# The order table of a one-core attention and MLP kernel, with its first three fifths ordered anew

## The chip, the core and the metric

The kernel runs on one core of one Trainium2 chip. The metric is the device time of one execution in microseconds (us). Five engines work side by side, each taking its own instructions strictly in the program's order: PE (TensorE, matmuls), ACT (ScalarE), DVE (VectorE), POOL (GpSimd, which here also issues one queue of transfers) and SP (SyncE, which issues the other transfers). They wait for each other by semaphores. The granted clock of PE is 1.00 in the profiled execution.

## The reference

q, k and v have shape (8, 8, 576, 64): 8 batches, 8 heads, 576 positions, 64 features. The attention is linear, and its output is the input x of a two-layer MLP with 4608 tokens, 512 inputs and 2048 hidden units.

```
q_s = softmax of q over its features
k_s = softmax of k over the positions
kv  = einsum('bhsd,bhse->bhde', k_s, v)
x   = einsum('bhsd,bhde->bhse', q_s, kv), reshaped to (4608, 512)
h   = x @ w_in
g   = h * tanh(softplus(h))
out = g @ w_out
```

## The kernel before

**What it computes, in which parts.** Item i (0 to 31) is a pair of heads of one batch; items 4b to 4b+3 make the 512 inputs of batch b. The first 512 positions of a batch are one column block of x, and the 64 left over from each of the 8 batches make a ninth. Every matmul of the MLP is done as three with operands split in a high and a low part (high by high, high by low, low by high), so each operand is first cast (high part) and then subtracted (low part).

Column blocks 0 to 2 go through the plain MLP. n = 0 to 47 is 16 hidden blocks for each of the three: `H` (four parts, or `HM`, all four) makes the first layer in bank ph, `Y` the activation, `G` or `GA` the high part gh (on DVE or on ACT), `GL` the low part gl (on DVE), `O` or `OP` the second layer in the banks po. Column blocks 3 to 8 go through it two at a time, in three passes k = 0, 1, 2, with seven products for eight: `A k.n.p` is product p (1 to 7) of hidden block n of the first layer (banks px, py, pz), `BB k.f.p` the same of the second layer (banks qx, qy, qz), six matmuls per step for `A` and six for `BB`. `C` copies a bank out on ACT (L860), `J` adds a bank to such a copy on DVE (L864), `N` is the activation. A bank is free for the next product when its `C`, `J` or `N` is done.

**Weights.** `R j` loads a weight tile; `RA`, `RM` or `RL` or `RS`, `RB`, `RC`, `RH` and `RO` or `RD` turn it into its high and low part on ACT, POOL and DVE. For the passes with seven products, weights are mixed (`WW`, `WM`), split (`WH`, `WL`) and put into the DRAM tensor ws by transfers on SP (`WP`, `WK`). `F e` fetches two of them back with one transfer of 512 KB on the POOL queue (L815) into one of six ring slots.

**Attention.** `LK`, `LQ` and `V` load k, q and v on SP. `MK` and `KA` take the maximum of k (DVE) and subtract it (ACT), `KT` transposes k on PE, `EK` is its exponential (ACT). `MQ`, `SQ`, `EQ`, `Q`, `QZ` and `QM` make the softmax of q on DVE, POOL, ACT, DVE, DVE and POOL; `T` transposes it and `TC` copies it out. `KP` multiplies k by v (`PK` later, together with the tails), `S` scales the product into kvt, `XP` or `PX` multiplies q by kvt. `ZT` copies the tail of an item out on ACT, `ST` stores it. `FI n` puts n fill matmuls on PE, whose results nobody reads; they stand at the start alone.

**What sets the order.** There is no scheduler. The string ORDER (L23 to L154) lists 2551 tokens, such as `KT1he` or `A0.2.7`: a step, its numbers, and letters that name its banks. The loop at L970 issues the steps one after the other, and what each issues stands on its engines' queues in that order. So a token's place decides what it stands behind on each of its engines, and its letters decide which bank it waits for.

```
for token in ORDER.split():
    name, numbers, letters = re.fullmatch("([A-Z]+)([0-9.]*)([a-z]*)", token).groups()
    stages[name](*(int(x) for x in numbers.split(".") if x), *([letters] if letters else []))
```

Of the kernel before, what the change touches and what calls it, by code (L numbers as in the profile page):

```python
# [24 lines left out]
V3 MQ2 FI1g FI9a EK1 R2 QZ0 SQ2 MK2 EQ1 V2 Q1 KA2 QM0 EQ2 KT2hd R3 QZ1 RA0b MQ3 QM1 R7 T0ge EK2 Q2 FI4a RM0 R10 SQ3
TC0 T1fc RB0 R4 KP0a QZ2 TC1 RC0 EQ3 QM2 R5 RA1d S0 RM1 LK4 MK3 XT0bc RH0 XP0ha Q3 KA3 R6 RL2 RD0 ZT1 KT3ef Z0 QZ3 R8
T2gc EK3 RB1 QM3 TC2 ZL0 KP2f LQ4 ZT0 RC1 Z1 RL3 ZL1 RH1 T3he PP RA2g S2 H0c TC3 ST1 RB2 RO1 H1 RA3d XP2ha RC2 R9 RB3
RH2 XT2eg H4b RC3 RO2 Z2 R11 Z3 H5 ZL2 RH3 RL7 ZL3 H6 RA7f L4 RM4 H8a MK4 ZT3 ZT2 RA4d RL5 H2 RD3 LK6 RA5g H3 LK5 RB4
RA6h H7 RL6 RC4 H9 R13 RB5 H12e Y0 R14 RC5 RL8 Y1 V4 H10 RB6 RA8d H13 RB7 RH5 R12 H11 RC6 GA0 RO5 H14 GL0 Y2 LQ5 RB8
H15 RH4 RL10 GA1 MQ4 H16h R17 Y3 RC8 H17 GA2 RO4 R16 GL1 RH6 H18 GL2 RA9g H19 RO6 RM9 RC7 O0 GA3 MK5 R19 Y4 RL13 R15  # L30
RB9 RA10f GL3 RM11 RH7 RC9 RA11e O1 RB10 RO7 RH9 RB11 RM14 RC10 RO9 GA4 RC11 RH8 R21 RH10 LK7 GL4 RO8 H20g R20 RH11
MQ5 RA13h B4e H21 KS4 RO10 RM12 H22 RA12f H23 SQ5 RB13 H24e RB12 SQ4 H25 RC12 EK4 H26 RC13 R23 RL16 EQ4 R22 H27 ST2
RH13 Q4 KP4fh EQ5 R24 RS17 R18 R30 O2 RO13 S4 ST0 Y5 R31 MK6 RO11 RA17f V6 RM15 G5 RH12 RB17 RL19 O3 Y6 RC17 RA14h GL5
# [1002 lines left out]
```

## Time and profile before

| what | before |
|---|---|
| median of 3 runs | 793.56 us (793.13 to 794.63) |
| the profiled execution | 795.84 us |
| its span, first to last instruction | 794.1 us |
| instructions in the span | 12637 |
| DMA | 178.85 MB, mean 225 GB/s |
| granted clock of PE | 1.00 in every stretch of 20 us but the last, partly empty one (0.94) |

The span leaves out what lies before the first and after the last instruction; 1.8 us of the profiled execution lie outside it. Times below are counted from the span's start. In rows of the timeline, the first number is the start in us, the second the length, then engine, line, operation, what is written and read, the shape, the count, and in brackets the idle time of the engine just before it and what ended it. A row of the waits has the waiting engine and line, what it waited for, the time in total, how often, and the longest.

### The profile page before, as it was taken

Reading aid. Unit: us, or ns where it says so; the run is one execution under the profiler, and the core shown is the slowest. Engines: PE = TensorE matmul, PEld = TensorE weight load, DVE = VectorE, ACT = ScalarE, POOL = GpSimd, SP = SyncE. Lnnn points to the kernel's source line nnn. Section 1 sums busy time; section 2 is a strip of 40 time slices with the busy share of each in tenths; the row PEclk is TensorE's granted clock in tenths of the full one; section 3 lists DMA queues with packets and bytes.
Section 4 is the critical chain, followed back from the end, with each engine's and each line's share of the span. In section 5 each row is a group of like instructions: output and inputs, shape, how many; then the busy total and the mean of one; then the engine's idle time right before and its main releaser. Section 6 shows DMA issues by size and latency. Waiting matters only on the chain.

```text
span 794.1 us, 12637 instructions
## 1 busy us (share of the span) xinstructions
PE 781.2 (98%) x4640; PEld 632.7 (80%) x4640; DVE 539.0 (68%) x877; ACT 498.4 (63%) x946; POOL 277.1 (35%) x350
## 2 busy tenths in 40 slices
PE   8999999999999999989999999999999999999997
PEld 7788868788878778867778788778878888888886
DVE  6997976777676778654789885335897822257854
ACT  6998857667685767379885653769654513446351
POOL 6998621432424444345232113412211212112111
PEclk9999999999999999999999999999999999999999
DMA  9994556847493556789766657785857776657576
GB/s 338 405 355 162 200 170 208 295 139 228 159 308 128 188 184 208 256 279 281 253 199 231 218 188 236 224 273 158 274 181 229 228 222 212 206 165 236 163 236 185
DMA packets 76684, 178.85 MB, mean 225 GB/s; under 512 B 15568, under 2 KB 28112, under 8 KB 76624
## 3 DMA queue, kind: packets, MB, share of 16 engines
q0 software_dynamic: 24768, 90.19, 35.7%
q1 hardware_dynamic: 51712, 87.74, 32.6%
q8 instruction: 36, 0.59, 0.3%
q14 instruction: 24, 0.20, 0.1%
q10 hardware_dynamic: 144, 0.13, 0.0%
HBM read 138.19 MB, written 39.85 MB: 224 GB/s over the span
## 4 chain that ended last, share of the span: by engine, by line
PE 86%; ACT 5%; DVE 3%; DMA 3%; issue 2%; POOL 0%; SPq 0%; DVEq 0%; ACTq 0%; POOLq 0%
PE ph L645 15%; PE po L683 14%; PE px L832 13%; PE qx L849 12%; PE qz L849 8%; PE qy L849 8%; PE py L832 7%; PE pz L832 3%; DMA ws<-m_out 2%; PE pt L567 1%; PE px L532 1%; DMA q<-in_q_dram 1%; ACT g L868 0%; DVE g L864 0%; ACT q L464 0%
## 5 line engine op out<-in xcount | busy, mean ns | idle before, releaser
L815 POOL DMA_DIRECT2D ws<-ws x172 | 92.8, 542 | 330.3 <-PE px L832 65.7
L882 ACT CAST gs<-g 128x1024 fp32r<-128x1024 f32 x84 | 86.9, 1050 | 70.4 <-PE qx L849 35.2
L832 PE MATMUL px<-xh,ws 128*128 128x512 f32 x384 | 129.7, 391 | 0.7 <-ACT g L860 0.6
L218 DVE TENSOR_TENSOR gs<-g,gs 128x1024 fp32r<-128x1024 f32 x84 | 102.1, 1232 | 34.1 <-ACT gs L882 34.1
L683 PE MATMUL po<-wo,gh 128*128 128x512 f32 x384 | 119.8, 393 | 0.0
L849 PE MATMUL qx<-gs,ws 128*128 128x512 f32 x432 | 101.8, 390 | 0.0
L849 PEld LDWEIGHTS qx<-gs,ws 128*128 128x128 f32 x432 | 80.8, 188 | 18.4 <-issue 1.6
L645 PE MATMUL ph<-xs,wi 128*128 128x512 f32 x384 | 92.5, 391 | 0.0
L860 ACT COPY g<-px 128x512 f32<-128x512 f32 x72 | 41.5, 586 | 75.7 <-PE px L832 75.6
L832 PEld LDWEIGHTS px<-xh,ws 128*128 128x128 f32 x384 | 72.1, 188 | 17.9 <-ACT g L860 1.8
L683 PEld LDWEIGHTS po<-wo,gh 128*128 128x128 f32 x384 | 71.1, 188 | 17.3 <-issue 1.6
L645 PEld LDWEIGHTS ph<-xs,wi 128*128 128x128 f32 x384 | 71.6, 188 | 16.0 <-ACT xt_first L617 0.8
L683 PE MATMUL po<-wo,gl 128*128 128x512 f32 x192 | 75.0, 391 | 0.0
L832 PE MATMUL px<-xl,ws 128*128 128x512 f32 x192 | 74.7, 389 | 0.0
L864 DVE TENSOR_TENSOR g<-py,g 128x512 f32<-128x512 f32 x48 | 32.7, 686 | 55.3 <-PE py L832 37.4
L832 PE MATMUL py<-xh,ws 128*128 128x512 f32 x192 | 66.8, 390 | 2.1 <-DVE g L864 2.1
L849 PE MATMUL qz<-gs,ws 128*128 128x512 f32 x288 | 67.5, 389 | 0.0
L849 PE MATMUL qy<-gs,ws 128*128 128x512 f32 x288 | 67.4, 389 | 0.0
L849 PEld LDWEIGHTS qy<-gs,ws 128*128 128x128 f32 x288 | 54.1, 188 | 11.2
L849 PEld LDWEIGHTS qz<-gs,ws 128*128 128x128 f32 x288 | 54.0, 188 | 11.2
L218 POOL TENSOR_TENSOR q<-q,qm 128x576 f32<-128x576 f32 (+1 forms) x32 | 39.2, 1227 | 54.3 <-DVE qm L377 32.9
L218 DVE TENSOR_TENSOR g<-g,g 128x1024 f32<-128x1024 f32 x48 | 57.3, 1214 | 0.2
(166 smaller groups left out, 1380.2 us busy)
## 6 DMA issues: line engine op xcount, KB each, us to landing
ws<-ws POOLq DMA_DIRECT2D x172, 512.0 KB, 4.6
v<-in_v_dram SPq DMA_DIRECT2D x14, 594.0 KB, 6.1
ws<-m_in SPq DMA_DIRECT2D x32, 256.0 KB, 3.0
ws<-m_out SPq DMA_DIRECT2D x32, 256.0 KB, 3.7
...
```

Source lines behind the costliest of these rows:

```text
L218: eng.tensor_tensor(out, a, b, ALU.subtract)
L532: nc.tensor.matmul((px, pt)[x][h][o], kvt[a, j], at[e + j]["qT"][x][a], start=True, stop=True)
L567: nc.tensor.matmul(pkv[i][j * D:(j + 1) * D], k, v_two[a, j, c], start=c == 0, stop=c == NR - 1)
L645: nc.tensor.matmul(gs[n], wi[f][:, a, t], x[:, z], start=t == 0 and i == 0, stop=t == HP - 1 and i == 2)
L683: nc.tensor.matmul(po[t], g[a][:, t * P:(t + 1) * P], wo[f][:, z], start=f == 0 and i == 0, stop=f == NF - 1 and i == 2)
L815: nc.gpsimd.dma_start(t.rearrange("p s z j c -> p s (z j c)"), ws[e % (NW // 2)].bitcast(F32R))
L832: nc.tensor.matmul(dst, w[:, a, j], xc[k, p][z][:, j].rearrange("p b s -> p (b s)"), start=p in (1, 2, 7) and j == 0 and i == 0, stop=j == ...
L849: nc.tensor.matmul(psb[key, k][m], w[:, a, m], g[:, z, f % 2], start=first and i == 0, stop=f == NH - 1 and i == 2, skip_group_check=p in ...
L860: nc.scalar.copy(g_quad(k, n)[q], psb[1, k, n])
L864: nc.vector.tensor_tensor(g, psb[2 if q == 0 else 7, k, n], g, ALU.add)
L882: nc.scalar.copy(t[:, 0], gq[k, h][G_PART[p]])
```

## The change

The string ORDER is replaced; nothing else is. Both strings have 2551 tokens. They hold the same steps with the same numbers, but for 69 tokens. Most of these have other bank letters. Twelve move the high part of a hidden block between engines (eight from DVE to ACT, four from ACT to DVE), and twelve move a step of the weights' conversion to another engine (`RL`, `RM`, `RS` for each other, `RO` and `RD` for each other). The last 446 tokens stand as before, and of the tokens before them nearly all stand elsewhere. The first lines of the string and of its common part show the kind of the difference:

```diff
-FI1h FI12a LK0 LQ0 LK1 LQ1 EX LQ2 LK2 LQ3 R0 LK3 MQ0 V0 V1 MK0 SQ0 MK1 R1 KA0 MQ1 KT0db EQ0 FI3a KA1 SQ1 Q0 EK0 KT1he
...
+FI1g FI1e FI9g LK0 LQ0 LK1 LQ1 EX LQ2 LK2 LQ3 MK0 V0 R0 KA0 KT0ba V1 MQ0 FI3c FI12f R1 MK1 SQ0 KA1 R2 MQ1 EQ0 KT1hg V2
...
```

The new string has one line more, so a line of the kernel's code is L(n+1) where it was L(n).

**PE at the start.** Its first rows before: fills (idle), then the transposes of k of items 0, 1 and 2 (pk, pkt), with fills in between.

```order
L407 MATMUL idle_127<-ident 128x128 x12
L435 MATMUL pk_171<-ident,kt_140 128x128 x4
L436 MATMUL pkt_172<-ident,kt_140 64x128
L407 MATMUL idle_179<-ident 128x128 x3
L435 MATMUL pk_189<-ident,kt_144 128x128 x4
L436 MATMUL pkt_190<-ident,kt_144 64x128
L407 MATMUL idle_199<-ident 128x128
L407 MATMUL idle_201<-ident 128x128 x9
```

The same rows of the change:

```order
L408 MATMUL idle_127<-ident 128x128
L408 MATMUL idle_129<-ident 128x128 x9
L436 MATMUL pk_159<-ident,kt_139 128x128 x4
L437 MATMUL pkt_160<-ident,kt_139 64x128
L408 MATMUL idle_169<-ident 128x128 x3
L408 MATMUL idle_173<-ident 128x128 x12
L436 MATMUL pk_196<-ident,kt_143 128x128 x4
L437 MATMUL pkt_197<-ident,kt_143 64x128
L408 MATMUL idle_206<-ident 128x128 x4
```

The twelve fills stand behind the first transposes now, and the group of one and nine that stood behind the second transposes stands ahead of the first.

**DVE between its work for ph12 and ph14**, ahead of KP6 on PE, which takes the bank of ph14. Before, from the low part of hidden block 12 to that of 14:

```order
L218 TENSOR_TENSOR gl12_1290<-ph12_1193,gh12_1279 128x512
L485 TENSOR_SCALAR qs6_1272,total6_1297<-qs6_1272 128x10
L486 RECIPROCAL qs6_1272<-qs6_1272 128x10
L377 TENSOR_TENSOR km8_1186<-km8_1186,kw8_1253 128x4
L485 TENSOR_SCALAR qs7_1260,total7_1306<-qs7_1260 128x10
L486 RECIPROCAL qs7_1260<-qs7_1260 128x10
L218 TENSOR_TENSOR gl13_1309<-ph13_1197,gh13_1300 128x512
L490 TENSOR_TENSOR q6_1058<-q6_1058,qs6_1272 128x640
L663 CAST gh14_1325<-ph14_1222 128x512
L263 SCALAR_TENSOR_TENSOR wc_out14_1295<-wc_out14_1295,raw_x_105 128x512
L218 TENSOR_TENSOR gl14_1332<-ph14_1222,gh14_1325 128x512
```

The same stretch of the change, with the five rows ahead of it:

```order
L742 TENSOR_TENSOR w_in1_1272<-wi1_90 128x512
L742 TENSOR_TENSOR w_in1_1272<-wi9_98 128x512
L264 SCALAR_TENSOR_TENSOR wc_out14_1259<-wc_out14_1259,raw_x_105 128x512
L271 SCALAR_TENSOR_TENSOR wc_out14_1259<-raw_x_105,wc_out14_1259 128x512
L219 TENSOR_TENSOR gl12_1298<-ph12_1206,gh12_1291 128x512
L491 TENSOR_TENSOR q6_1021<-q6_1021,qs6_1237 128x640
L476 TENSOR_REDUCE qs7_1318<-q7_1087 128x10
L486 TENSOR_SCALAR qs7_1318,total7_1327<-qs7_1318 128x10
L487 RECIPROCAL qs7_1318<-qs7_1318 128x10
L219 TENSOR_TENSOR gl13_1332<-ph13_1195,gh13_1323 128x512
L219 TENSOR_TENSOR gl14_1335<-ph14_1227,gh14_1325 128x512
```

The cast gh14, the join of km8, the reciprocal of q6 and a weight step no longer stand between gl12 and gl14; two weight steps and w_in1 stand ahead of gl12.

**DVE ahead of the product py of hidden block 4 in pass 0** (A0.4.7), whose bank is that of block 2 and is free when both additions from py0_2 are done (J). qm24 is the maximum of item 24, whose load is LQ24. Before:

```order
L377 TENSOR_TENSOR qs23_4073<-qs23_4073,sz23_4091 128x18
L485 TENSOR_SCALAR qs23_4073,total23_4106<-qs23_4073 128x18
L486 RECIPROCAL qs23_4073<-qs23_4073 128x18
L386 TENSOR_REDUCE qm24_4122<-q24_4075 128x18
L864 TENSOR_TENSOR g0_1_0_3921<-pz0_3_4018,g0_1_0_3921 128x512
L864 TENSOR_TENSOR g0_1_2_3923<-py0_2_3892,g0_1_2_3923 128x512
```

The change:

```order
L865 TENSOR_TENSOR g0_1_3_3921<-py0_2_3906,g0_1_3_3921 128x512
L458 STREAM_TRANSPOSE k24_4111<-kt_two_114 128x576
L865 TENSOR_TENSOR g0_2_0_4079<-pz0_4_4113,g0_2_0_4079 128x512
L865 TENSOR_TENSOR g0_1_2_3920<-py0_2_3906,g0_1_2_3920 128x512
L387 TENSOR_REDUCE qm24_4151<-q24_4075 128x18
```

The addition from py0_2 stands ahead of the maximum of item 24 now, where it stood two rows behind it.

**Fetches.** Two places of the string, from a fetch to the step that first reads it. Before, with BB0.3.1 the first that reads F30 and BB0.5.2 the first that reads F36:

```
F30 GK0.1.0 N0.1.3 A0.6.3 C0.7.2 T25 MS26 GX0.0.0v A0.7.5 N0.6.1 J0.7.0 A0.6.4 GX0.0.1v N0.7.0 N0.1.2 C0.7.3 MT26 BB0.0.1 SQ26
F32 BB0.1.1 GX0.1.0v F33 GK0.1.2 EQ26 BB0.2.1 F34 LQ27 J0.7.3 ST22 BB0.3.1
F36 J0.7.2 N0.7.3 F35 GX0.3.0v QW26 F37 PK24df GK0.2.1 N0.5.2 KB28 PX24cb J0.6.2 GH0.2.2 BB0.6.1 QV26 N0.6.3 MQ27 N0.4.3
GK0.2.2 BB0.0.2 N0.6.2 XR25 GX0.2.0v N0.7.2 BB0.1.2 MS27 MT27 BB0.7.1 SQ27 GH0.7.0 XR24 GK0.7.0 BB0.2.2
...
```

The change:

```
F33 T25 F30 S24 F31 BB0.0.1 F32 J0.6.2 EQ26 GK0.1.3 BB0.1.1 C0.7.3 LQ27 GK0.1.2 BB0.2.1 Q26 BB0.3.1
F39 XR25 GK0.2.2 MS27 F36 BB0.2.2 XR24 T26 KB28 GK0.2.3 BB0.3.2 XH1.1 F40 GX0.1.1v GH0.7.0 BB0.4.2 KM28 GH0.7.1 GK0.7.0 BB0.5.2
```

More of the change, by code (lines that the diff above doesn't have):

```diff
@@ L23 @@
 ORDER = """
-FI1h FI12a LK0 LQ0 LK1 LQ1 EX LQ2 LK2 LQ3 R0 LK3 MQ0 V0 V1 MK0 SQ0 MK1 R1 KA0 MQ1 KT0db EQ0 FI3a KA1 SQ1 Q0 EK0 KT1he
[L25 to L33, printed above, removed]
@@ L89 @@
-EQ25 A0.6.6 F26 LQ26 Q25 WP15.0 PS GH0.1.1 J0.4.2 A0.5.4 U26.0 N0.4.1 A0.5.3 J0.5.2 C0.6.2 GK0.1.1 QW25 A0.6.5 F29
-N0.4.2 J0.6.0 N0.5.0 QV25 A0.6.7 GH0.1.2 U26.1 N0.1.0 MQ26 LK28 A0.7.1 N0.0.0 F28 V26 A0.7.2 C0.7.0 GH0.1.0 A0.7.7 F31
-C0.6.3 QM25 N0.2.3 J0.6.3 N0.0.3 A0.7.6 N0.6.0 F30 GK0.1.0 N0.1.3 A0.6.3 C0.7.2 T25 MS26 GX0.0.0v A0.7.5 N0.6.1 J0.7.0
-A0.6.4 GX0.0.1v N0.7.0 N0.1.2 C0.7.3 MT26 BB0.0.1 SQ26 F32 BB0.1.1 GX0.1.0v F33 GK0.1.2 EQ26 BB0.2.1 F34 LQ27 J0.7.3
-ST22 BB0.3.1 Q26 N0.5.3 MK28 GH0.1.3 BB0.4.1 N0.5.1 GX0.1.1v GH0.2.0 A0.7.4 GH0.2.1 GK0.2.0 A0.7.3 GK0.1.3 BB0.5.1
@@ L94 @@
-N0.7.1 F36 J0.7.2 N0.7.3 F35 GX0.3.0v QW26 F37 PK24df GK0.2.1 N0.5.2 KB28 PX24cb J0.6.2 GH0.2.2 BB0.6.1 QV26 N0.6.3
-MQ27 N0.4.3 GK0.2.2 BB0.0.2 N0.6.2 XR25 GX0.2.0v N0.7.2 BB0.1.2 MS27 MT27 BB0.7.1 SQ27 GH0.7.0 XR24 GK0.7.0 BB0.2.2
-F39 DP0.0.0 F38 DP0.0.1 KM28 GH0.2.3 QM26 BB0.3.2 F40 GX0.2.1v BB0.4.2 GH0.7.1 GK0.2.3 BB0.5.2 F41 GX0.3.1v BB0.6.2
-T26 GK0.7.1 BB0.7.2 EQ27 BB0.0.7 GH0.7.2 Q27 LQ28 GX0.0.2v BB0.1.7 GH0.7.3 F43 F42 GX0.1.2v BB0.2.7 GH0.6.0 GK0.7.2
-QW27 BB0.3.7 GK0.7.3 XH1.1 BB0.4.7 GH0.6.1 GX0.2.2v BB0.5.7 GX0.3.2v F45 F44 GK0.6.0 BB0.6.7 GH0.6.2 GX0.0.3v BB0.7.7
@@ L99 @@
-F46 DJ0.0.0 BB0.0.6 GK0.6.1 QV27 BB0.1.6 GK0.6.2 BB0.2.6 GH0.3.0 DJ0.0.1 QM27 DS0.0.1 GH0.6.3 BB0.3.6 ST23 F47 F48 V28
-GK0.6.3 DS0.0.0 BB0.4.6 GH0.5.0 GK0.3.0 BB0.5.6 F49 GX0.2.3v BB0.6.6 GH0.5.1 S26 T27 ZT24 UE28.1 BB0.7.6 F50 GX0.1.3v
-BB0.0.3 DP0.2.0 MQ28 ZT25 DP0.2.1 GK0.5.0 UE28.0 BB0.1.3 GH0.5.2 XL1.1 PX26df GH0.5.3 GK0.5.1 BB0.0.5 XR26 U28.0 XR27
-XA1.0v XH1.3 BB0.1.5 F52 GK0.5.2 BB0.2.5 GH0.3.1 XA1.1v BB0.3.5 F53 GK0.5.3 F51 BB0.4.5 GH0.3.2 U28.1 GX0.3.3v XH1.5
-BB0.5.5 GK0.3.1 BB0.6.5 XL1.5 BB0.7.5 GK0.3.2 BB0.2.3 DP0.1.0 GH0.3.3 BB0.3.3 F56 XH1.2 GK0.3.3 F54 DP0.1.1 F55
@@ L104 @@
-BB0.4.3 XL1.3 GH0.4.0 XH1.7 DJ0.3.1 BB0.5.3 F57 XL1.2 BB0.6.3 GH0.4.2 XL1.7 GH0.4.1 BB0.7.3 GK0.4.2 F58 DJ0.3.0 A1.0.2
-GH0.4.3 DJ0.1.0 DS0.3.0 ST24 MS28 GK0.4.0 PK26df GK0.4.1 A1.0.1 XA1.2v BB0.0.4 GK0.4.3 XH1.6 BB0.1.4 C1.0.0 XL1.6 F59
-BB0.2.4 DJ0.1.1 J1.0.0 MT28 BB0.3.4 F60 SQ28 A1.0.7 F62 EQ28 Q28 LQ29 BB0.4.4 LK30 XA1.3v DS0.3.1 BB0.5.4 F61 A1.0.6
-A1.1.1 C1.0.2 XH1.4 A1.0.5 XL1.4 BB0.6.4 C1.0.3 S28 MQ29 BB0.7.4 F64 J1.0.3 MS29 F63 MK30 A1.0.3 QW28 F65 C1.1.0
-DJ0.2.0 A1.0.4 QV28 A1.1.6 J1.0.2 A1.1.2 C1.1.2 KB30 A1.1.5 J1.1.0 F66 DJ0.2.1 A1.2.7 MT29 C1.1.3 QM28 F68 A1.2.1 KM30
@@ new lines @@
+EK0 FI4e MQ2 SQ1 LK3 EK1 Q0 SQ2 V3 EQ1 MK2 R3 QZ0 KA2 Q1 QM0 EQ2 KT2de R4 RM0 QZ1 R5 MQ3 RA0h QM1 T0fb EK2 RB0 LK4
+RA1d Q2 SQ3 T1ag RM1 RC0 KP0e TC1 QZ2 TC0 RB1 R8 EQ3 RL2 S0 RH0 MK3 R6 XT0cb XP0ha R7 Q3 KA3 QM2 ZT1 ZT0 KT3fg QZ3 R10
+Z0 RD0 T2bc EK3 RC1 QM3 Z1 KP2f ZL0 TC2 ZL1 RA2g R9 RL3 T3hd PP RH1 S2 H0c TC3 RB2 R11 H1 RA3a RO1 RC2 RM4 XP2he RB3
+ST1 RH2 RC3 RO2 R13 XT2df H4b Z2 ZT3 H5 Z3 ZL2 RL5 LQ4 ZT2 RA4g ZL3 H2 RH3 RB4 H3 RA5f L4 MK4 RL8 H8e RC4 H6 LQ5 RD3
+RL6 H7 Y0 RB5 RA6h H9 LK6 RC5 RA7a H10 RL7 LK5 RB6 GA0 H12f RH5 GL0 RA8d H11 R15 RC6 RO5 RH4 R12 H13 RB8 Y1 H14 R30
@@ new lines @@
+A0.7.2 WP15.0 PS GH0.1.0 ZT23 N0.3.0 LK28 N0.6.0 A0.5.4 ST23 GH0.1.1 F28 ST22 MQ26 A0.7.1 C0.6.3 V26 J0.5.2 N0.4.3
+J0.6.3 MS26 A0.6.3 GK0.1.1 C0.7.0 N0.5.0 A0.6.4 GK0.1.0 N0.4.2 GH0.1.2 J0.7.0 A0.7.6 N0.5.1 MT26 SQ26 N0.6.1 N0.7.0
+A0.7.7 C0.7.2 QM25 GH0.1.3 A0.7.5 F33 T25 F30 S24 F31 BB0.0.1 F32 J0.6.2 EQ26 GK0.1.3 BB0.1.1 C0.7.3 LQ27 GK0.1.2
+BB0.2.1 Q26 BB0.3.1 J0.7.3 QW26 QV26 A0.7.3 GX0.1.0v N0.6.2 A0.7.4 N0.6.3 MK28 QM26 N0.1.3 N0.5.2 F34 BB0.4.1 GX0.0.0v
+N0.5.3 F35 N0.0.3 N0.7.3 BB0.5.1 GX0.0.1v F37 N0.2.2 N0.7.1 MQ27 BB0.6.1 N0.2.3 J0.7.2 GH0.2.0 GX0.3.0v BB0.7.1 N0.7.2
@@ new lines @@
+F38 N0.3.2 GK0.2.0 PK24df GH0.2.3 GX0.3.1v DP0.0.0 PX24cb DP0.0.1 GX0.2.0v GH0.2.1 BB0.0.2 GH0.2.2 GK0.2.1 BB0.1.2 F39
+XR25 GK0.2.2 MS27 F36 BB0.2.2 XR24 T26 KB28 GK0.2.3 BB0.3.2 XH1.1 F40 GX0.1.1v GH0.7.0 BB0.4.2 KM28 GH0.7.1 GK0.7.0
+BB0.5.2 F41 ZT24 MT27 GX0.2.1v BB0.6.2 GK0.7.1 GH0.7.2 BB0.0.7 SQ27 BB0.1.7 F42 GX0.1.2v GX0.0.2v BB0.2.7 EQ27 UE28.0
+LQ28 GK0.7.2 BB0.3.7 GH0.6.0 GX0.2.2v BB0.4.7 GH0.6.1 GK0.6.1 BB0.7.2 F45 F44 GK0.6.0 BB0.5.7 GH0.7.3 F43 GK0.7.3
+BB0.0.6 GH0.6.2 ZT25 GX0.3.2v BB0.6.7 Q27 BB0.1.6 U28.0 F46 QW27 XL1.1 BB0.7.7 QV27 GK0.6.2 BB0.2.6 GH0.6.3 GH0.3.0
@@ new lines @@
+GK0.6.3 BB0.3.6 MQ28 QM27 BB0.4.6 S26 F47 DJ0.0.1 BB0.5.6 F48 T27 DJ0.0.0 BB0.6.6 GH0.5.1 GX0.3.3v DS0.0.0 DS0.0.1
+GH0.5.0 BB0.7.6 V28 GK0.3.0 MS28 PX26df GH0.5.2 MT28 XA1.0v BB0.0.3 XR26 GK0.5.2 DP0.2.0 GK0.5.0 BB0.1.3 DP0.2.1 XR27
+SQ28 XH1.3 BB0.0.5 GH0.5.3 F49 GK0.5.1 BB0.1.5 F50 F52 GX0.0.3v BB0.2.5 GH0.3.1 GK0.5.3 BB0.3.5 F53 GX0.1.3v F51
+BB0.4.5 GX0.2.3v GH0.3.2 XH1.2 GK0.3.2 BB0.5.5 UE28.1 GK0.3.1 BB0.6.5 XH1.5 U28.1 GH0.3.3 BB0.7.5 XL1.3 BB0.2.3
+DP0.1.0 DP0.1.1 EQ28 DJ0.3.1 BB0.3.3 F56 LQ29 DJ0.3.0 F55 LK30 XL1.2 F54 BB0.4.3 DS0.3.0 GH0.4.1 GK0.3.3 GH0.4.0
@@ new lines @@
+BB0.5.3 F57 GK0.4.0 PK26df GH0.4.2 GK0.4.1 BB0.6.3 S28 GK0.4.2 BB0.7.3 F58 XA1.1v BB0.0.4 XA1.2v BB0.1.4 F59 DJ0.1.0
+XH1.6 XA1.3v BB0.2.4 XH1.7 XL1.6 A1.0.1 F60 XL1.5 BB0.3.4 C1.0.0 DJ0.1.1 GH0.4.3 XL1.7 A1.0.6 GK0.4.3 A1.0.7 C1.0.2
+A1.1.1 A1.0.2 A1.0.5 F62 BB0.4.4 C1.0.3 XH1.4 BB0.5.4 F61 C1.1.0 XL1.4 BB0.6.4 J1.0.3 MK30 BB0.7.4 F64 F63 A1.0.3
+DJ0.2.0 F65 Q28 A1.0.4 J1.0.0 QW28 QV28 A1.1.6 MQ29 J1.0.2 MS29 A1.1.2 C1.1.2 KB30 A1.1.5 J1.1.0 F66 DJ0.2.1 A1.2.7
+MT29 C1.1.3 QM28 F68 A1.2.1 KM30 T28 SQ29 A1.1.7 C1.2.0 F70 EQ29 A1.1.3 LQ30 J1.1.3 ST24 Q29 DS0.3.1 N1.0.1 A1.2.6
@@ new lines @@
+BB2.3.5 F165 F164 GK2.5.3 BB2.4.5 GK2.3.1 BB2.5.5 BB2.6.5 GH2.3.3 GH2.3.2 BB2.7.5 F167 F166 GK2.3.2 BB2.2.3 GH2.4.0
+DP2.1.0 GK2.4.0 BB2.3.3 DP2.1.1 GX2.3.3v BB2.4.3 GH2.4.1 GK2.3.3 BB2.5.3 F169 DJ2.3.0 DJ2.3.1 BB2.6.3 GH2.4.2 BB2.7.3
+F170 BB2.0.4 DJ2.1.1 GH2.4.3 GK2.4.1 BB2.1.4 F171 DJ2.1.0 F168 GK2.4.3 DS2.1.0 BB2.2.4 DS2.3.0 DS2.1.1 GK2.4.2 DS2.3.1
+BB2.3.4 BM2.4.4.0 BM2.5.4.0 BM2.6.4.0 BM2.7.4.0 DJ2.2.0 DS2.2.0 BM2.4.4.1 BM2.5.4.1 BM2.6.4.1 BM2.7.4.1 DK2.2.1.0
+DT2.2.1.0 DK2.2.1.1 DT2.2.1.1
```

200 lines of the change are left out of this document (100 added, 100 removed).

## The prediction

> **What bounds the kernel now.** I read the page's shares first, then the waits of the tensor engine, then busy time by stretches, then single rows at the places that the change touches.
>
> ```profile
> PE 781.2 (98%) x4640; PEld 632.7 (80%) x4640; DVE 539.0 (68%) x877; ACT 498.4 (63%) x946; POOL 277.1 (35%) x350
> ...
> PE 86%; ACT 5%; DVE 3%; DMA 3%; issue 2%; POOL 0%; SPq 0%; DVEq 0%; ACTq 0%; POOLq 0%
> ```
>
> PE is busy 98% of the span and makes 86% of the chain that ended last. The change neither adds nor removes a matmul, and pairs of small matmuls (64 rows) stand beside each other as often as before, so the 781.2 us stay. What can move is PE's idle time, 794.1 - 781.2 = 12.9 us. The waits of PE and the busy time by stretches (columns: stretch, length, busy us of PE, PEld, DVE, ACT and POOL, clock, DMA) say where it lies:
>
> ```profile
> PE py L832 <- DVE g L864: 2.1, 1, 2.1
> ...
> PE pkv L567 <- DVE gl L218: 1.3, 1, 1.3
> ...
> PE px L832 <- ACT g L860: 0.6, 1, 0.6
> PE px L532 <- ACT odd L617: 0.5, 1, 0.5
> ...
> 0.00:22.00 22.00, 18.16 (x197) 16.40 (x197) 14.98 (x36) 16.03 (x35) 14.19 (x20) 1.00 0.93 345
> 22.00:95.00 73.00, 73.00 (x414) 58.70 (x412) 66.04 (x110) 63.53 (x116) 62.43 (x48) 1.00 0.75 278
> ...
> 450.00:780.00 330.00, 330.00 (x1615) 271.07 (x1615) 194.96 (x234) 172.75 (x269) 72.39 (x127) 1.00 0.67 212
> 780.00:794.00 14.00, 9.68 (x43) 7.69 (x41) 4.97 (x7) 0.00 (x0) 1.06 (x2) 0.99 0.65 207
> ```
>
> From 22 to 95 us and from 450 to 780 us PE never idles. The last 4.3 us are the end of the store, which keeps its order. The start holds 3.8 us, and four single waits hold 2.1 + 1.3 + 0.6 + 0.5 = 4.5 us, all between 95 and 450 us, inside the part that is ordered anew. So the change is the sum of three terms: how much later or earlier the steady stream of matmuls begins, what of the four waits goes, and what new waits come.
>
> **Term 1, the start.** PE's rows (start, length, what, count, and in brackets the idle time before):
>
> ```profile
> 1.65 4.68 PE L407 MATMUL idle<-ident 128*128 128x128 f32 x24
> 7.83 0.74 PE L435 MATMUL pk<-ident,kt 128*128 128x128 f32 x4 [1.50 <-ACT kt L429]
> ...
> 8.52 0.83 PE L407 MATMUL idle<-ident 128*128 128x128 f32 x6
> 9.20 0.75 PE L435 MATMUL pk<-ident,kt 128*128 128x128 f32 x4
> ...
> 9.89 2.40 PE L407 MATMUL idle<-ident 128*128 128x128 f32 x20
> 12.12 0.70 PE L435 MATMUL pk<-ident,kt 128*128 128x128 f32 x4
> ...
> 14.85 1.39 PE L548 MATMUL pkv<-v,k 128*64 128x66 f32 x40
> 17.12 0.27 PE L532 MATMUL pt<-kt_two,kvt 64*64 64x64 f32 x2 [0.88 <-DVE kvt L599]
> ...
> 21.98 1.64 PE L645 MATMUL ph<-xs,wi 128*128 128x512 f32 x6
> ```
>
> The first load of k, kt0 (issue, then the time to landing):
>
> ```profile
> L332 SPq DMA_DIRECT2D kt<-in_kt_dram x1: 383/383/383, 0.7 to 0.7; - x1
> ...
> DMA to landing us min/median/max: 2.9/2.9/2.9
> ```
>
> A fill shows as two matmul rows. Before, 26 rows of fills stand ahead of the first transposes of k (KT0) and 6 between the first and the second (KT1). After, 22 and 30. The 26 ended at 1.65 + 4.68 = 6.33; four fewer, at 0.11 us each, and the last one's tail of 0.2 off, PE is free for KT0 near 5.7 us. KT0 also needs the maximum and the subtraction of kt0, which landed at 0.7 + 2.9 = 3.6 us and which no longer stand behind the maximum of q0: 3.6 and two steps of 0.8 us at most give 5.2, so KT0 starts at 5.7 us. The step from KT0 to the fills takes 0.69 (7.83 to 8.52, as 9.20 to 9.89), and a fill takes (12.12 - 9.89) / 20 = 0.11 us. So KT1 starts at 5.7 + 0.69 + 30 x 0.1115 = 9.74 instead of 9.20: the 1.50 us that PE waited are spent on fills, and 0.54 us more. Who stands behind KT1:
>
> ```profile
> 9.98 0.60 ACT L441 ACTIVATE k<-pk 128x512 f32<-128x512 f32 x1 [0.19 <-PE pk L435]
> ...
> 11.39 0.82 DVE L475 TENSOR_REDUCE qs<-q 128x10 f32<-128x640 f32 x1 [0.40 <-ACT q L464]
> ...
> 12.81 1.26 POOL L490 TENSOR_TENSOR q<-q,qs 128x640 f32<-128x640 f32 x1 [0.20 <-DVE qs L486]
> ...
> 14.46 0.70 DVE L263 SCALAR_TENSOR_TENSOR wa<-wa,raw_x 128x512 uint32<-128x512 uint32 x1 [0.39 <-ACT raw_x L251]
> ...
> 16.29 0.16 DVE L597 TENSOR_SCALAR rs<-pkv 128x2 f32<-128x2 f32 x1 [0.27 <-PE pkv L548]
> ```
>
> EK1 waits for KT1, the exponential of q1 stands behind EK1 on ACT, Q1 waits for that, QM1 for Q1's reciprocal, T1 for QM1, and the first k-by-v product KP0 for T1 on PE. Each row shows that its wait ended there, so 0.54 us pass through to KP0 (15.39). Then the normalised product S0 goes 16.29 to 16.83 by the chain, but in the new order DVE has one weight step more (RB1) ahead of S0. RB0 can start no earlier than now, 14.4, since ACT does RM0 and RA0 after the later exponentials; from there RB0, Q2, RC0, QZ2 and RB1 take 0.60 + 0.73 + 0.60 + 0.40 + 0.60 by the spacing of such rows (14.46 to 15.06 is the first), which puts S0 at 17.3. That is 1.0 us later; the first product with it (17.12) and, since the maximum of k3 (MK3), its subtraction and KT3, KP2 stand behind S0 on their engines, the first matmuls of the first layer (21.98 now) move with it. **I take +1.0 us.** A gain is excluded, because KT1 stands behind the 30 fills on PE itself; the ends are +0.5 (only the fills) and +1.6 (another step on DVE or ACT in the way). The cover is thin: PE has no idle row from 22 to 95 us in which it could make up for it.
>
> **Term 2, the four waits.** The 2.1 us at 352 us:
>
> ```profile
> 352.34 0.75 DVE L386 TENSOR_REDUCE qm<-q 128x18 f32<-128x576 f32 x1 [4.46 <-DMA q<-in_qs_dram]
> 353.01 0.68 DVE L864 TENSOR_TENSOR g<-pz,g 128x512 f32<-128x512 f32 x1
> 353.60 0.68 DVE L864 TENSOR_TENSOR g<-py,g 128x512 f32<-128x512 f32 x1
> ...
> 354.34 0.50 PE L832 MATMUL py<-xh,ws 128*128 128x512 f32 x1 [2.11 <-DVE g L864]
> ```
>
> DVE sat 4.46 us on a load of q24 with the two additions behind it that empty the bank for py of block 4. In the new order both additions stand ahead of that reduction, and between the load's issue and its use stand six A steps instead of three, at the 1.36 us below. This wait goes whole. DVE's rows around the 1.3 us at 102 us, ACT's at 391 and 447 us, and a step of six matmuls of the second layers' kind:
>
> ```profile
> 97.73 0.68 DVE L218 TENSOR_TENSOR gl<-ph,gh 128x512 fp32r<-128x512 f32 x1
> ...
> 103.01 0.68 DVE L218 TENSOR_TENSOR gl<-ph,gh 128x512 fp32r<-128x512 f32 x1
> ...
> 391.28 0.58 ACT L860 COPY g<-px 128x512 f32<-128x512 f32 x1
> ...
> 447.50 0.22 ACT L617 COPY odd<-pt 128x64 f32<-128x64 f32 x1
> ...
> 645.52 1.36 PE pz L832 x6
> ```
>
> The 1.3 us is KP6 waiting for the low part of ph14: before, nine rows of DVE lie between gl12 (97.73) and gl14 (103.01), after five; the two reciprocal rows of q6, the join of km8, the cast gh14 (now on ACT) and one weight step are gone from between them and a sum of q7 has come in, 1.6 us less by their spacing, but w_in1 and two further steps are put ahead of gl12. I leave 0.3 us of it. The 0.6 us at 391 us is A0.7.5 behind a copy on ACT; its copy now stands one A step earlier, but a cast that needs the landing of the last mixed weights stands before it, and these are stored later: I leave 0.2. The 0.5 us at 447 us is a copy of a tail (ZT25) behind a copy that waited for a store; the tail's copy now stands far ahead: gone. **Term 2: -(4.5 - 0.5) = -4.0 us**, ends -4.5 and -2.5. DVE loses four casts and one weight step and ACT gains about five, 0.6 us each; both have 30% idle, so I cost that at nothing, and between 22 and 95 us (DVE 66 of 73 us busy) at up to 1 us, which is in the ends.
>
> **Term 3, new waits.** Weights of the last two fifths of the layers come back from DRAM by fetches on the POOL queue (issues of tile ws, then the time to landing):
>
> ```profile
> L815 POOL DMA_DIRECT2D ws<-ws x3: 535/537/547, 404.9 to 405.9; - x3
> ...
> DMA to landing us min/median/max: 3.5/4.5/6.6
> ```
>
> ```profile
> L815 POOL DMA_DIRECT2D ws<-ws x9: 527/567/591, 326.8 to 348.8; - x9
> ...
> DMA to landing us min/median/max: 3.5/7.6/8.0
> ```
>
> Of three issued together the first lands after 3.5 us, the second 4.5, the third 6.6; where stores and loads run beside them the median is 7.6. In the new order F30 and F36 have three steps of PE (4.1 us) between issue and use, where they had six and more; F8, F18, F49, F61 and F62 have four, 5.4 us. F30 stands right behind F33 and F36 just behind F39: second ones, 4.5 us and a little more: 0.6 us each. The others stand alone or first: 3.5 to 4.5, hidden. **I take +1.2 us**, ends 0 (all land like first ones) and +6 (all land like the median of the crowded stretch, 7.6, with the seven waits sharing half).
>
> **Sum.** +1.0 - 4.0 + 1.2 = -1.8 us. The profiled execution took 795.84 us (span 794.1 and 1.8 around it) and would take 794.0; the median of the runs shown is 793.56, 2.3 below it, and the difference carried over gives **791.8 us**. A measurement of this kernel tells about 0.2%, 1.6 us, from no change, so the forecast lies just past that bound.
>
> **Rivals.**
> Holes for holes (chance 0.30): the fetches and loads whose lead was cut take back what the old waits gave, about 3 us in place of 1.2. For it: four waits of this kind came up in the old order too; against it, F fetches are spread wider between 320 and 350 us than before. Time: +1.0 - 4.0 + 3 = 0, 793.6, no change.
> Crowded fetches (0.18): slower. The seven short fetches all land as in the second fence above, 7 to 8 us. By the row's 7.6, those with 5.4 us lose 2.2 and those with 4.1 lose 3.5; where one wait also covers the next (F61 and F62) they count once, some 5.5 to 6 us in all. It decides from 1.0 - 4.0 + x > 1.6, that is x > 4.6. At 5.5 the time is 796.1. Against it, the shortest leads stand after 380 us, where the DMA is less full. [...]
> Cold fills (0.04): were the 30 fills to run as slowly as the first 24 (4.68 / 24 = 0.195 us), KT1 would be 2.5 us later still, and the time 794.3. Against it, the fills before and after the 1.50 us gap ran at 0.11. [...]
> All goes well (0.10): the start costs only the fills, the waits go whole, nothing new: +0.5 - 4.5 + 0.2, 789.8.
>
> **How the numbers follow.** The forecast has 0.38; with "all goes well" faster by over 0.2% gets 0.48; "holes for holes" and half of the cold case give 0.32 within 0.2%; the crowded case and the rest 0.20 slower. The range goes from 789.2 (start +0.5, waits -4.5, nothing new, and the 0.4 us by which the fastest of the runs shown lies below their median) to 795.6 (crowded to 5 us), leaving out most of the crowded case's upper half.
>
> **What would show it.** KT1 at 9.7 and the first product of the first layer about 1 us later than 21.98; no wait of py for DVE near 352 us and none of px for the tail's copy; waits of PE for ws landings at F30 (product BB0.3.1) and F36 (BB0.5.2) under 1 us each. It is wrong if the stream starts at 22 us or before, if PE waits for fetches by more than 3 us in all, or if an engine off PE's path stalls on a load with an emptying copy behind it, as DVE did at 352 us.

## The result, and the profile after

| kernel | median of its runs | range of its runs | ratio to before | 95% interval |
|---|---|---|---|---|
| before | 793.56 us | 792.99 to 794.84 | 1 | |
| the change | 801.95 us | 797.99 to 804.67 | 1.0101 | 1.0066 to 1.0135 |

The change makes the kernel slower by 8 us, and the time lies 6 us above the upper end of the forecast's range. Here and below, four executions of 866.8 us and more were slow ones and are left out of every median and ratio. The profiled execution took 801.38 us, its span is 799.6. From the page of the changed kernel, the span and PE's busy time:

```profile
span 799.6 us, 12643 instructions
PE 783.7 (98%) x4640; PEld 634.6 (79%) x4640; DVE 540.6 (68%) x872; ACT 501.0 (63%) x951; POOL 280.3 (35%) x350
```

The span grew by 5.5 us. PE's idle time went from 12.9 to 799.6 - 783.7 = 15.9 us, and PE's busy time grew by 2.5 us although it does the same 4640 matmuls. So there are two losses to find: 3.0 us of waiting (more waits came than went), and matmuls that took longer. (The medians differ by 8.4 us, more than the spans, because the profiled execution of before was 2.3 us above its median and that of the change 0.6 under.)

The waits of PE in the changed kernel:

```profile
PE px L833 <- ACT g L861: 2.9, 1, 2.9
PE px L833 <- ACT raw L782: 2.5, 1, 2.5
PE pk L436 <- ACT kt L430: 1.3, 2, 1.1
PE pt L533 <- ACT q L465: 1.2, 1, 1.2
...
PE qx L850 <- DVE gs L219: 0.8, 1, 0.8
...
PE ph L646 <- DVE gl L219: 0.5, 1, 0.5
...
PE pt L568 <- DMA v<-in_v_dram: 0.3, 1, 0.3
PE qz L850 <- DMA ws<-ws: 0.2, 1, 0.2
```

Gone are py's 2.1 us for DVE, pkv's 1.3 and px's 0.5 for the tail's copy. Fetched weights (ws) cost 0.2 us. But two single waits of px for ACT stand on top, where one of 0.6 us stood. Two short waits for DVE are new as well, 0.5 us of ph (at 70 us) and 0.8 of qx (at 454 us); they stand with 0.5 to 0.6 and 0.7 to 0.8 us in every trace of the new order below, and in none of the old one. The busy time by stretches says where the slow matmuls are (columns as in the prediction); first two stretches of before, then the change:

```profile
340.00:400.00 60.00, 57.23 (x327) 45.42 (x326) 37.15 (x75) 51.10 (x103) 24.24 (x33) 1.00 0.87 277
400.00:450.00 50.00, 49.53 (x295) 38.74 (x294) 44.03 (x58) 32.09 (x57) 12.81 (x19) 1.00 0.68 224
```

```profile
95.00:340.00 245.00, 244.42 (x1765) 195.18 (x1764) 176.93 (x360) 166.83 (x379) 95.52 (x106) 1.00 0.64 207
340.00:400.00 60.00, 54.59 (x309) 43.58 (x308) 33.28 (x70) 46.22 (x93) 19.85 (x29) 0.96 0.88 271
400.00:450.00 50.00, 49.76 (x295) 39.74 (x297) 42.53 (x56) 32.88 (x59) 13.96 (x18) 0.98 0.58 184
```

The slow matmuls and the largest waits lie between 340 and 450 us: PE idles 5.4 us in the first 60 of these (2.8 before), and the granted clock falls to 0.96 and 0.98. Now the rows at the two waits, in the order of their engines. DVE, then ACT, then PE at the first wait:

```profile
367.43 0.75 DVE L387 TENSOR_REDUCE qm<-q 128x18 f32<-128x576 f32 x1 [2.82 <-DMA q<-in_qs_dram]
...
368.27 0.85 ACT L374 COPY sm<-qm 32x18 f32<-32x18 f32 x4 [3.45 <-DVE qm L387]
369.15 0.59 ACT L782 COPY raw<-px 128x512 f32<-128x512 f32 x1
...
369.79 0.50 PE L833 MATMUL px<-xh,ws 128*128 128x512 f32 x1 [2.55 <-ACT raw L782]
```

The load of q25 had not landed. DVE's maximum (MQ25) waited for it, ACT's copy of the maxima (MS25) waited for DVE, and behind that, on ACT's queue, stood XR22, which has nothing to do with q25 but empties the bank that PE's next product needs. It is the stall of 352 us in the old order again, one engine further on. ACT and PE at the second wait, the first six matmuls behind it and the 24 after those, and 24 of the same kind later:

```profile
393.15 1.05 ACT L883 CAST gs<-g 128x1024 fp32r<-128x1024 f32 x1 [2.41 <-DMA ws<-m_out]
...
395.59 0.58 ACT L861 COPY g<-px 128x512 f32<-128x512 f32 x1
...
396.23 0.79 PE L833 MATMUL px<-xh,ws 128*128 128x512 f32 x1 [2.86 <-ACT g L861]
...
398.95 7.18 PE L850 MATMUL qx<-gs,ws 128*128 128x512 f32 x24
...
408.69 5.60 PE L850 MATMUL qx<-gs,ws 128*128 128x512 f32 x24
```

The cast GH0.1.2 waited for the landing of the last mixed weights, and the copy C0.7.2 (395.59) stood behind it and three activations. Then the matmuls were slow: 2.72 us from 396.23 to 398.95 for six that take 6 x 5.60 / 24 = 1.4 at full speed, and 7.18 instead of 5.60 for the next 24, together 2.9 us. That accounts for the 2.5 us of busy time that PE gained. The landing times of the two, before and after (last mixed weights by L719, L720; q25 by L340, L341):

```profile
L719 SPq DMA_DIRECT2D ws<-m_out x2: 385/404/422, 378.6 to 379.0; - x2
...
DMA to landing us min/median/max: 6.0/6.1/6.2
```

```profile
L720 SPq DMA_DIRECT2D ws<-m_out x2: 319/372/424, 384.2 to 384.6; - x2
...
DMA to landing us min/median/max: 8.3/8.4/8.5
```

```profile
L340 SPq DMA_DIRECT2D q<-in_qs_dram x1: 342/342/342, 362.2 to 362.2; - x1
...
DMA to landing us min/median/max: 3.4/3.4/3.4
```

```profile
L341 SPq DMA_DIRECT2D q<-in_qs_dram x1: 333/333/333, 360.5 to 360.5; - x1
...
DMA to landing us min/median/max: 6.9/6.9/6.9
```

The weights' stores were issued 5.6 us later and took 2.3 us longer. The load of q25 took 6.9 us instead of 3.4, and DVE came to its use 4.1 us after the issue (367.43 - 2.82 - 360.5). So the shorter lead alone doesn't make this wait: with the 3.4 us of before, the load would have landed 0.7 us ahead of DVE.

The longer landings belong to the new order, not to one execution. In the three traces that have the old order at this place (before, and e11 and e12 below) q25 landed after 2.9 to 3.9 us and the last mixed weights after 5.6 to 6.2; in the twelve that can be read of the new order q25 took 4.8 to 7.2 and the slower of the two stores 7.8 to 8.9. What in the new order makes them longer, no run here separates.

### The profile page after: what moved, and what is told of

It is laid out like the page before. It is cut to its first block, busy times and chain, and to the rows that moved or that the text cites. A ratio compares the mean times of both kernels' runs of the same rounds, so it can differ in the third digit from the quotient of the medians.

```text
span 799.6 us, 12643 instructions
## 1 busy us (share of the span) xinstructions
PE 783.7 (98%) x4640; PEld 634.6 (79%) x4640; DVE 540.6 (68%) x872; ACT 501.0 (63%) x951; POOL 280.3 (35%) x350
## 4 chain that ended last, share of the span: by engine, by line
PE 87%; DVE 4%; ACT 4%; DMA 3%; issue 1%; POOL 0%; DVEq 0%; SPq 0%; ACTq 0%
PE ph L646 15%; PE po L684 15%; PE px L833 14%; PE qx L850 11%; PE qy L850 8%; PE qz L850 7%; PE py L833 6%; PE pz L833 3%; PE pt L568 2%; PE px L533 1%; PE idle L408 1%; DMA ws<-m_out 1%; DMA q<-in_qs_dram 1%; DMA v<-in_v_dram 1%; DVE gs L219 1%
## 5 line engine op out<-in xcount | busy, mean ns | idle before, releaser
L219 POOL TENSOR_TENSOR q<-q,qm 128x576 f32<-128x576 f32 (+1 forms) x32 | 41.3, 1293 | 37.0 <-DVE qm L378 15.5
```

Source lines behind the costliest of these rows:

```text
L219: eng.tensor_tensor(out, a, b, ALU.subtract)
```

## The experiments

Theory A: the two ACT copies behind late transfers, and the slow matmuls behind the waits, are the loss. Theory B: the late landing of the last mixed weights holds the whole stretch, and moving copies doesn't help. Theory C: the loss is spread over many small waits. Every ratio below is to the kernel before, timed beside it on the same chip; 0.0010 is 0.8 us. A difference of two ratios has the errors of both: by the intervals some 1 us among e5 to e8, 1.6 between these and e3, 2.3 between e2 and e3, and 3 and more against the change's first timing.

**One repair each, and both.** e1 puts XR22 ahead of MS25, e2 puts the cast behind the copy, e3 does both.

```diff
-MQ25 PK22df MS25 F23 XR22 MT25
+MQ25 PK22df XR22 MS25 F23 MT25
...
-GH0.1.2 J0.7.0 A0.7.6
+J0.7.0 A0.7.6
...
-C0.7.2 QM25 GH0.1.3 A0.7.5
+C0.7.2 QM25 GH0.1.2 GH0.1.3 A0.7.5
```

> The changed kernel with one token moved: the copy of px of item 22 on ACT (XR22) stands ahead of the copies for the maximum of item 25 (MS25), which wait for a load. Theory A (two copies that empty banks stand behind a wait on ACT, at 367 and 393 us, and the second wait costs a spell at half the TensorE clock besides): the wait of 2.5 us at 367 us goes to under 0.3, the one at 393 us stays at 2.9, as its chain moves along with PE; time 802 - 2.5 = 799.5. Theory B (the landing of the last mixed weights, not PE, sets when the stretch ends): the wait at 393 us grows by what the first one loses, to about 5.4, and the time stays at 802. Theory C (many small waits all over, or the start): the time stays within 1 us of 802 although the wait is gone.

> The changed kernel with one token moved: the cast of the first layer's output that waits for the last mixed weights' store (GH0.1.2) stands behind the copy C0.7.2 on ACT. Theory A: the wait of 2.9 us ahead of A0.7.5 falls to about 0.3, the 2.7 us of matmuls at half clock behind it go, mean clock 1.000; time 802 - 5.3 = 796.7. Theory B: the landing still holds the stretch; the wait turns up at the first matmul that reads that cast (BB0.4.1) and the time stays above 800. Theory C: within 1 us of 802.

> Both moves together. Theory A: both waits and the slow spell go: 802 - 2.5 - 5.3 = 794.2, mean clock 1.000. Theory B: no better than the second move alone. Theory C: within 1 us of 802.

| kernel | median | ratio | 95% interval |
|---|---|---|---|
| e1_copy_ahead | 800.12 us | 1.0064 | 1.0038 to 1.0090 |
| e2_cast_behind | 798.69 us | 1.0042 | 1.0018 to 1.0065 |
| e3_both | 797.32 us | 1.0024 | 1.0008 to 1.0041 |

Against the change's 1.0101 these are 2.9, 4.7 and 6.1 us; the intervals of e2 and e3 lie apart from the change's, that of e1 overlaps it. Moving one copy and one cast gives back some three quarters of the loss. That goes against C, and e2, under 800 us without a new wait at BB0.4.1, goes against B as the main cause. But A as I had put it was too small a picture. The waits of PE in e1, and then in e3:

```profile
PE px L833 <- ACT g L861: 4.3, 2, 2.6
PE pt L568 <- DMA v<-in_v_dram: 1.4, 1, 1.4
```

```profile
PE pt L568 <- DMA v<-in_v_dram: 2.1, 1, 2.1
PE px L833 <- ACT g L861: 1.7, 1, 1.7
```

With XR22 out of the way, the next copy behind MS25 (C0.4.2) holds PE instead, 1.7 us in both. And a third late load shows, V22, ahead of the product PK20: it cost 0.3 us in the profiled execution of the change and 1.1 to 2.1 in the other traces that have it at its place (1.4 in e1, 2.1 in e3). In e2 the wait at 393 us is gone, and the slow matmuls now stand behind the other wait. PE of e2:

```profile
370.57 0.79 PE L833 MATMUL px<-xh,ws 128*128 128x512 f32 x1 [2.77 <-ACT raw L782]
371.16 0.63 PE L833 MATMUL px<-xl,ws 128*128 128x512 f32 x1
371.59 1.05 PE L833 MATMUL px<-xh,ws 128*128 128x512 f32 x2
```

So they don't belong to a place in the program. Where they come, they follow a wait.

**The rest of the stall, and the third load.** On e3, e5 issues V22 early, e6 takes MS25 and MT25 behind three copies, e7 does both. e8 is e7 with the first 46 tokens (and RB1) in the order of before.

```diff
-WW14v V22 ES2.1
+WW14v ES2.1
...
-OP46.2 C0.0.3
+OP46.2 V22 C0.0.3
...
-XR22 MS25 F23 MT25 QV24
+XR22 F23 QV24
...
-A0.4.5 C0.6.0 A0.5.5
+A0.4.5 C0.6.0 MS25 MT25 A0.5.5
```

> The two moved copies of e3_both, and the load of v for pair 22 issued early, some 22 us of TensorE's work ahead of its product as in the kernel before, instead of 4. Theory A (named stalls on late loads, and the half-clock spell that an idle wait sets off): the wait of 2.1 us of the first product of heads 20 to 23 goes and the short half-clock spell of about 0.9 us behind it, so the time falls by about 3 us under that of e3_both (797.3), to 794 to 795, the level of the kernel before. Rival C (the difference is spread out, and the early load only pushes the mixed-weight fetches beside it back by its 594 KB): the wait goes, waits of 0.5 us and more for fetched weights come between 322 and 335 us, and the time stays within 1 us of 797.3.

> The two moved copies of e3_both, and the ACT copy that stands behind the late load of q for pair 25 (and its maximum) moved behind the emptying copies C0.4.2, C0.5.2 and C0.6.0. Theory A: TensorE's wait of 1.7 us at 371 us goes and nothing takes its place, so 1.5 to 2 us less than e3_both: 795.3 to 796. Rival (a hole only moves, as it did from e1_copy_ahead's first to its second copy): another wait of 1 us and more stands between 366 and 380 us, now for the maxima themselves or for the next product of heads, and the time stays within 0.5 us of 797.3.

> e5 and e6 together: four repairs of named stalls. Theory A: no wait of TensorE over 1 us is left between 330 and 400 us, the granted clock there is 0.99 or more, and the time is 792 to 793.5, at or a little under the kernel before. Rival C: 795 to 797.

> e7 with the first 46 tokens in the order of before (fills, first loads and k products) and RB1 behind S0 again. Theory A with the start as predicted (+0.9 us in the trace of after): the first layer-one product is issued at 22.0 instead of 22.9 us, and the time is 0.7 to 1.1 us under e7's. Rival: the start's loss is taken up by a wait further on, and the time is that of e7 within 0.3 us.

| kernel | median | ratio | 95% interval |
|---|---|---|---|
| e5_v_early | 796.27 us | 1.0023 | 1.0011 to 1.0034 |
| e6_max_late | 795.29 us | 1.0009 | 0.9998 to 1.0019 |
| e7_both_late | 794.28 us | 0.9996 | 0.9988 to 1.0005 |
| e8_start_back | 794.58 us | 1.0002 | 0.9992 to 1.0011 |

e7 stands level with before: four groups of moved tokens undo the whole loss. The maxima are worth 1.2 us (e6 against e3, within the errors) to 2.1 (e7 against e5), about as A said. The early load of v alone gave 0.1 us where A expected 3; the wait is gone from its trace, but its executions spread from 793.3 to 798.2 us, and beside the other repair it is worth 1.0 (e7 against e6), no more than the errors. I can't say where it went in e5. PE's waits in e7 show what is left:

```profile
PE qz L850 <- DMA ws<-ws: 1.1, 1, 1.1
...
PE qy L850 <- DMA ws<-ws: 1.0, 1, 1.0
```

With a third of 0.3 (qx) these are 2.4 us of waits for fetched weights, where the profiled execution of the change had 0.2. e8 was a miss: the time is e7's within the errors. Its first product of the first layer starts at 22.71, against 23.21 in e7 and 21.98 before, but a single trace can't tell such a step: with the start of the change unaltered, that product came between 21.95 (e3) and 23.37 (e14) in eleven traces. The spread begins at the first fills, whose group of twenty rows took 3.73 us in e3 and 4.62 in the change.

**The change's own terms, one by one, on the kernel before.** e11 gives it the start of the change alone (fills and the order of the first 46 tokens, but not all of its bank letters). e12 moves one token, the maximum behind which two additions stood at 352 us:

```diff
-MQ24 UE24.0 J0.3.0 C0.3.2 A0.2.4 A0.3.5 J0.2.2 N0.2.1 WL14.1 A0.4.7
+UE24.0 J0.3.0 C0.3.2 A0.2.4 A0.3.5 J0.2.2 N0.2.1 WL14.1 MQ24 A0.4.7
```

> The kernel before, with the start of the change alone (the fills and the order of the first 46 tokens). As predicted: the first layer-one product 0.5 to 1.6 us later than 21.98 and the time 0.5 to 1 us over before. Rival (a later wait takes the start up, as e8_start_back against e7 may have shown): within 0.3 us of before.

> The kernel before, with one move: the maximum MQ24, which waits for the late load of q on DVE, stands behind three additions and a weight cast instead of ahead of them. As predicted for this wait (whole): TensorE's 2.1 us at 352 us go and the time falls by 2.1 us. Rival (Holes for holes): the same 2 us come back as waits for fetched weights or for ACT copies before 500 us, and the time stays within 0.6 us of before.

| kernel | median | ratio | 95% interval |
|---|---|---|---|
| e11_start_alone | 795.76 us | 1.0018 | 1.0009 to 1.0027 |
| e12_one_gain_alone | 792.83 us | 0.9976 | 0.9963 to 0.9988 |

The start of e11 costs 1.4 us (0.7 to 2.1), so nothing later takes it up whole. In e11's trace the first product of the first layer starts at 23.84, 1.9 us later than before and later than in any trace of the change's own start. A wait of fills for ACT (0.73 us at 12.6 us) stands ahead of it that neither before nor the change has, and the wait of py at 355 us is 1.4 us where before had 2.1. So 1.4 us is rather an upper figure for the start of the change. The one wait is worth 1.9 us (1.0 to 2.9), as the prediction said of it (2.1), and the time says that little of it comes back elsewhere, though short new waits stand in its trace (up to 0.5 us, px for fetched weights). DVE of e12 at that place, where the maximum no longer waits:

```profile
352.64 0.68 DVE L219 TENSOR_TENSOR m_out<-m_out 128x512 fp32r<-128x512 f32 x1
353.24 0.74 DVE L387 TENSOR_REDUCE qm<-q 128x18 f32<-128x576 f32 x1
```

This kernel of one moved token beats both, the one before and the change.

**Waits, or slow matmuls behind them?** Four kernels ask how much of the loss is the clock. e4 and e13 are the change with fill matmuls in the second wait, so that PE isn't idle there; e14 is the change itself, on e13's chip. e9 is e7 with the cast ahead of the copy again, e10 is e9 with the fills.

```diff
-C0.7.2 QM25 GH0.1.3 A0.7.5
+C0.7.2 QM25 GH0.1.3 FI12h A0.7.5
```

> The changed kernel with 12 fills (24 matmul rows of 0.11 us, 2.6 us of PE) put on PE directly ahead of A0.7.5, in bank h, so that PE works through its wait at 393 us; nothing else is moved, the results of the fills are read by nobody. If the slow matmuls after 396 us come from PE's idling (theory A): the wait stays (A0.7.5 still starts near 396.2) but the matmuls after it run at 0.227 us instead of 0.427, mean clock 1.000, time 802 - 2.7 = 799.3. If they come from something else, such as the transfers at that place: the clock stays at 0.995 and the time at 802.

> The kernel of e7_both_late with one repair taken back: the cast GH0.1.2, which waits for the landing of the last mixed weights, stands ahead of the copy C0.7.2 on ACT again. Theory A: one wait of TensorE of 2.4 to 3 us near 390 us, followed by 13 matmuls or so at 427 instead of 227 ns (2.7 us), so 4.5 to 6 us over e7. Rival D (the half clock of the earlier traces came from something else, such as a hot stretch, and the wait alone is lost): 2.4 to 3 us over e7, granted clock 1.00 behind the wait.

> e9 with twelve idle matmuls of the kernel's own kind (the ones that fill the start) written in the wait, ahead of A0.7.5, in a bank that is free there; they cost about 1.3 us of the wait itself. Theory A: the wait stands as in e9 but the clock stays at full speed behind it, so the time is 2.4 to 3 us over e7 and 2 to 3 us under e9. Rival D: the same time as e9 within 0.5 us.

> The changed kernel with twelve fill matmuls ahead of A0.7.5, as in e4_fills_in_wait, beside the changed kernel itself on the same chip (e14_after_again). Theory A: the wait for the copy C0.7.2 stands, but the matmuls behind it run at 227 ns instead of 427, so the time is 2 to 3 us under that of e14. Rival D (the slow matmuls have another cause, or come in few executions only): the time is within 0.8 us of e14's.

> The changed kernel unaltered: 1.0066 to 1.0135 times before, as in its first timing, the two waits of 2.5 us and more at 370 and 396 us, and behind one of them matmuls at 427 ns. If the executions differ in the granted clock (1.000 against 0.995), those with 1.000 are 3 us and more faster.

| kernel | median | ratio | 95% interval |
|---|---|---|---|
| e4_fills_in_wait | 800.17 us | 1.0068 | 1.0047 to 1.0089 |
| e9_stall_alone | 795.15 us | 1.0017 | 1.0002 to 1.0031 |
| e10_stall_filled | 798.01 us | 1.0034 | 1.0020 to 1.0047 |
| e13_fills_again | 798.76 us | 1.0069 | 1.0052 to 1.0086 |
| e14_after_again | 800.88 us | 1.0090 | 1.0069 to 1.0111 |

e4 has no trace that can be used; its ratio agrees with e13's. The fills take 2.1 us off the change (798.76 against 800.88; 1.7 by the ratios), within what A said, though the intervals of the two ratios overlap. The other pair has the same side, 1.0068 (e4) against the change's 1.0101. PE of e13, with the fills (24 rows, 2.84 us) where the wait was, and PE of e14:

```profile
392.54 2.84 PE L408 MATMUL idle<-ident 128*128 128x128 f32 x24
395.13 0.48 PE L833 MATMUL px<-xh,ws 128*128 128x512 f32 x1
...
396.59 5.60 PE L850 MATMUL qx<-gs,ws 128*128 128x512 f32 x24
```

```profile
371.20 0.50 PE L833 MATMUL px<-xh,ws 128*128 128x512 f32 x1 [2.19 <-ACT raw L782]
...
372.48 1.01 PE L833 MATMUL px<-xh,ws 128*128 128x512 f32 x2
...
398.33 0.50 PE L833 MATMUL px<-xh,ws 128*128 128x512 f32 x1 [2.05 <-ACT g L861]
...
399.84 7.24 PE L850 MATMUL qx<-gs,ws 128*128 128x512 f32 x24
```

With the wait filled, the 24 matmuls take 5.60 us; without, 7.24, and in e14 the same happens a second time behind the other wait. (In e13's trace that other wait was 0.5 us with no edit there, so the two traces differ by more than the fills.) The executions agree: those of the change and of e14 with a granted clock of 0.995 or 0.996 took 801.1 to 804.7 us, those with 0.998 to 1.000 took 797.99 to 800.67.

e9 and e10 told less. e9 is 1.7 us over e7, and its trace shows the wait (2.25 us) with the clock at full speed behind it, so A's 4.5 to 6 us didn't come (two of its executions, with a clock of 0.998 and 0.997, took 798.0 and 798.7 us, the others 793.5 to 796.6); e10 is 3.0 us over e7, in A's range for it, but above e9 instead of under. In e10 the fills cover nearly all of a longer wait:

```profile
390.80 2.84 PE L408 MATMUL idle<-ident 128*128 128x128 f32 x24
393.88 0.50 PE L833 MATMUL px<-xh,ws 128*128 128x512 f32 x1 [0.24 <-ACT g L861]
```

The wait was 2.84 + 0.24 = 3.1 us there and 2.25 in e9, from one landing to the next. So this pair says what the wait costs alone (1.7 and 3.0 us) and nothing on the clock.

## Why the prediction was wrong

**Term 1, the start (+1.0): right as far as the runs can tell.** The second transposes came at 10.07 where 9.74 was worked out (9.20 before), the first product of the first layer at 22.87 for 21.98, 0.9 us later. That the one trace agrees so well is partly luck, given the spread from 21.95 to 23.37; e11's 1.4 us in the time (0.7 to 2.1), with a wait of its own in it, covers the +1.0.

**Term 2, the four waits (-4.0): right for three, wrong for the fourth.** The waits at 352, 102 and 447 us went as said, and e12 shows that the largest of them is worth its length. The step that failed is "a cast that needs the landing of the last mixed weights stands before it, and these are stored later: I leave 0.2". The cast and the later store were seen, but no landing time was worked out for the 0.2. With the 6.1 us of before, the store issued at 384.6 would have landed at 390.7, just when ACT came to the cast (393.15 - 2.41 = 390.74): no margin at all. It took 8.4, and the 2.3 us of difference became the cast's wait of 2.41 whole; the copy came 2.86 us late for PE, and e2, which moves only this cast, gives back 4.7 us.

**Term 3, new waits (+1.2): the fetches were right in size, the list was not.** Fetched weights cost 0.2 us in the change's profile, 1.6 in that of the same kernel in e14 and 2.4 in e7's, on both sides of 1.2. But the term looked for shortened leads among the fetches alone. The loads of q25 and v22 were moved towards their uses too (q25's had one A step ahead in place of three and landed 2.8 us after DVE was ready for it, v22 had 4 us of PE's work ahead in place of 22), and ACT's copies behind MS25 were never looked at. Beside e2's repair, XR22 is worth 1.4 us (e3 against e2, within the errors), the maxima and v together 2.2 (e7 against e3). Nor were the two short waits for DVE on the list, 1.3 us together. The prediction's last line even named the event, "an engine off PE's path stalls on a load with an emptying copy behind it", and took it as a thing to watch for, not one to search the new order for.

**What no term had: a wait can cost more than its length.** PE's idle time was priced at its own length throughout, and "the 781.2 us stay" didn't hold: PE was busy for 783.7. In the profiled execution of the change, 2.9 us were lost to half-speed matmuls behind one wait, and e13 puts the share of that in the median at some 2 us, not clear of the errors. The rival "Cold fills" had looked for slow matmuls at the start alone (its thirty fills ran at 3.51 / 30 = 0.12 us, so it didn't come). The gap that it named lasted 1.50 us, and no slow fills came behind it (0.11 us each); the waits here that were followed by 427 ns matmuls lasted 2.05 us (e14) to 2.86 (the change), so that gap told nothing of them.

**The rivals.** "Crowded fetches" (0.18) had the side and, at 796.1, not the size; transfers did land later, but those of q25 and of the last mixed weights, not the fetches that it named. "Holes for holes" (0.30) named loads whose lead was cut beside the fetches, and at +3 was too small. Put together, the terms come near: start +1.4 (e11), three waits -3.9, fetches +2.4 (e7's trace) make -0.1, and e7, which has none of the large new waits, measured -0.3 (-1.0 to +0.4). The 1.3 us of short waits for DVE are left out of that sum, so it is near and not exact. From e7 to the change, the cast (4.7, e2), XR22 (1.4) and the maxima and v (2.2) add up to 8.3; they are steps from one of these kernels to the next, so that they make up the whole is arithmetic. So the terms that were priced came to about nothing, and the loss is in what was not priced, or at 0.2.
